# Agent attention with a token expert on one core: rank triangles made on GpSimd, ten key tiles, and a new order of the program

## The chip, the core and the metric

The kernel runs on one core of a Trainium2 chip. The metric is the device time of one execution in microseconds; of the kernel before there are three runs, and the changed kernel is compared with it by such runs. Engines are named as in the profile: PE (TensorE matmul), PEld (its weight load), DVE (VectorE), ACT (ScalarE), POOL (GpSimd), SP (SyncE, which here issues nearly all transfers).

## The reference

Four batches of 12608 tokens with 128 channels pass through agent attention with 49 agents, and then the 128 best tokens of each batch pass through an expert.

```python
def sm(a, b):
    s = scale * (a @ b.transpose(0, 2, 1))
    s = s - s.max(-1, keepdims=True)
    e = np.exp(s)
    return e / (e.sum(-1, keepdims=True) + 1e-09)
a2k = sm(agents, k)              # 49 x 12608
agent_v = a2k @ v                # 49 x 128
q2a = sm(q, agents)              # 12608 x 49
x = q2a @ agent_v                # 12608 x 128
...
scores = np.einsum('bsd,d->bs', x, w_gate)
out = x.copy()
for b in range(B):
    top_idx = np.argpartition(-scores[b], capacity)[:capacity]   # capacity = 128
    xe = x[b, top_idx]
    h = np.maximum(xe @ w1, 0.0)          # w1: 128 x 1024
    ye = h @ w2                           # w2: 1024 x 128
    g = 1.0 / (1.0 + np.exp(-scores[b, top_idx]))
    out[b, top_idx] = x[b, top_idx] + g[:, None] * ye
```

## The kernel before

**Tiles and stages.** Each batch is cut into seven chunks of tokens, six of 1920 and one of 1152. For a chunk of keys the transposed keys (`xT_b_c<-kT`) are loaded, and PE multiplies them with the agents (`S`, eight f32 matmuls of 480 columns, each counted twice in the trace, since an f32 matmul runs as two). DVE transposes the result into a key tile `sk` and takes the maximum `mx`. When all seven chunks of a batch are there, POOL subtracts the maximum and ACT takes the exponential in place, in `sk`. Then the values `v_b_c` are loaded and PE sums `sk` times `v` over the batch (`av`, one PSUM bank for each batch); `v_finish` divides and splits the result into fp16 halves `ws` (its matmuls are `pw` and `pp`). For the queries the transposed chunk is loaded and scored in the same way (`S`, DVE `sq` and `qm`); POOL, ACT, POOL make fp16 halves `f`, PE turns them (`fT`), ACT copies them out (`ft`), PE computes the gate scores (`pg`). When a batch is gated, its 128 best tokens are found and ranked: DVE and ACT count (`gt`) and PE broadcasts and sums (`all`, `pc`). The output is `po`, PE's product of `ft` and `ws`, four tokens of a partition at a time; DVE, ACT or ACT and POOL move it into `og_b_c`, which one transfer stores. The expert of batches 0 to 2 and that of batch 3 run among the last outputs (`ph`, `py`), and an indirect transfer writes their rows over the stored output.

**What sets the order.** Nothing is scheduled by the compiler. Every operation is recorded (`Recorder`), and `ORDER`, a list of 1466 numbers in lines 252 to 327, says in which order the operations are issued; `place` only asserts that each comes behind what it depends on. So the list sets, for each engine, the order of its instructions, and for SP the order of transfers. In the trace every such instruction has the line of that loop, L1123.

**Buffers.** All loads of k, q and v take a slot of the pool `inp` (`N_IN = 6`). A load is issued on SP when PE has done its last matmul on the tile that had the slot before, and whatever stands behind it on SP waits with it. Key tiles `sk` take a slot of `skp` (`N_SK = 9`), as do the two large pieces of the expert's weights (`w1_held`, `w2_held`) and the turned queries of batch 3. The outputs of batch 0 (`FILL`) have two slots of their own (`N_OG = 2`); the other 21 outputs use the six slots of `inp` once the loads have left them, and a new `og` waits there until the store of the `og` before it has landed.

**Constants.** `cst` is one transfer of 128x562 f32 (tenth on SP); a block of 128 columns in it is `tri`, ones above the diagonal. DVE casts it to bf16 as `tri_b` (L456), and adds the identity for `tri_i` (L462). Both serve only in the ranking of the best tokens, as weights of `pc`. `wg_sb`, the gate's vector, is the thirtieth transfer on SP, and `v_finish` is its first user; the matmul `pw` there is the first to use `cst` on PE.

```python
def load(src, name, w):
    t = inp.tile([P, TMAX * (C + 1)], F32, tag="in", name=name)
    nc.sync.dma_start(t[:, :w], src)
...
s = skp.tile([P, TMAX, AP_], F32, tag="sk", name=f"sk_{b}_{c}")
...
order, done = [rec.ops[i] for i in ORDER], set()
```

Of the kernel before, what the change touches and what calls it, by code (L numbers as in the profile page):

```python
# [24 lines left out]
P = 128  # L25
# [33 lines left out]
N_SK = 9  # L59
# [46 lines left out]
class Recorder:  # L106
# [1095 lines left out]
```

## Time and profile before

| | |
|---|---|
| runs | 287.15, 287.21 and 285.31 us, median 287.15 us |
| profiled execution | 285.31 us, span 283.4 us, granted clock 0.993 |
| busy, share of the span | PE 91%, PEld 62%, DVE 80%, ACT 60%, POOL 65% |
| moved | 106.68 MB, mean 376 GB/s |

The profiled execution is the fastest of the three. The span runs from its first to its last event; the 1.9 us between span and time lie around it. A name such as `v_2_1` means batch 2, chunk 1; the trace leaves the numbers out, the order of the program has them.

### The profile page before, as it was taken

Reading aid. Unit: us, or ns where it says so; the run is one execution under the profiler, and the core shown is the slowest. Engines: PE = TensorE matmul, PEld = TensorE weight load, DVE = VectorE, ACT = ScalarE, POOL = GpSimd, SP = SyncE. Lnnn points to the kernel's source line nnn. Section 1 sums busy time; section 2 is a strip of 40 time slices with the busy share of each in tenths; the row PEclk is TensorE's granted clock in tenths of the full one; section 3 lists DMA queues with packets and bytes.
Section 4 is the critical chain, followed back from the end, with each engine's and each line's share of the span. In section 5 each row is a group of like instructions: output and inputs, shape, how many; then the busy total and the mean of one; then the engine's idle time right before and its main releaser. Section 6 shows DMA issues by size and latency. Waiting matters only on the chain.

```text
span 283.4 us, 8570 instructions
## 1 busy us (share of the span) xinstructions
PE 258.7 (91%) x3524; PEld 175.7 (62%) x3524; DVE 226.3 (80%) x517; ACT 171.3 (60%) x313; POOL 183.8 (65%) x152
## 2 busy tenths in 40 slices
PE   1866699999999999999999999999999999999991
PEld 0211236556555756464575955866987989889980
DVE  0799999987999988999948979766954889997630
ACT  1103148454249965466685987998998865965510
POOL 1219699984489996358988418999426242568751
PEclk9999999999999999999999999999999999999997
DMA  7999999999999999999999999999644999899980
GB/s 278 426 424 417 421 423 415 418 421 421 417 419 417 398 416 418 383 384 417 421 423 416 378 423 425 411 408 421 208 198 139 344 376 411 351 415 380 417 332 27
DMA packets 18204, 106.68 MB, mean 376 GB/s; under 512 B 2032, under 2 KB 3440, under 8 KB 18160
## 3 DMA queue, kind: packets, MB, share of 16 engines
q1 hardware_dynamic: 17760, 105.42, 91.9%
q8 instruction: 30, 0.49, 0.7%
q0 software_dynamic: 256, 0.52, 0.6%
q10 hardware_dynamic: 144, 0.13, 0.1%
q14 instruction: 14, 0.11, 0.1%
HBM read 79.85 MB, written 26.21 MB: 374 GB/s over the span
## 4 chain that ended last, share of the span: by engine, by line
PE 64%; DMA 17%; DVE 9%; issue 3%; POOL 3%; ACT 1%; POOLq 0%; DVEq 0%
PE S L1123 23%; PE po L1123 13%; PE av L1123 10%; DMA v<-va 9%; DMA xT<-kT 6%; PE fT L1123 5%; PE pg L1123 3%; PE all L1123 3%; PE py L1123 3%; PE ph L1123 2%; DVE gt L1123 2%; DMA ag_sb<-agT 2%; DVE sk L1123 2%; DVE sq L1123 2%; DVE qm L1123 1%
## 5 line engine op out<-in xcount | busy, mean ns | idle before, releaser
L1123 PE MATMUL S<-xT,ag_sb 128*32 128x480 f32 (+1 forms) x896 | 97.8, 557 | 14.1 <-DMA ag_sb<-agT 6.1
L1123 POOL TENSOR_TENSOR sq<-sq,qm 128x735 f32<-128x735 f32 (+1 forms) x42 | 57.1, 1365 | 32.6 <-DVE qm L1123 31.1
L1123 PEld LDWEIGHTS <-ft 128*128 128x128 f16 x1188 | 57.9, 97 | 9.3 <-issue 8.4
L1123 PEld LDWEIGHTS S<-xT,ag_sb 128*32 128x32 f32 x896 | 24.4, 110 | 60.3 <-issue 25.8
L1123 POOL TENSOR_TENSOR f<-sq,f 128x735 f16<-128x735 f32 (+1 forms) x28 | 42.7, 1526 | 18.9 <-ACT f L1123 16.3
L1123 PE MATMUL po<-ws,ft 128*128 128x128 f16 x792 | 52.4, 219 | 0.5 <-ACT x L1123 0.4
L1123 ACT COPY ft<-fT 128x896 f16<-128x896 f16 (+2 forms) x49 | 42.9, 894 | 13.9 <-PE fT L1123 13.9
L1123 POOL TENSOR_TENSOR sk<-sk,mb 128x735 f32<-128x735 f32 (+1 forms) x28 | 47.3, 1701 | 6.2 <-DVE rs L1123 5.3
L1123 PE MATMUL av<-v,sk 128*64 128x129 f32 x792 | 47.8, 274 | 1.1 <-DMA v<-va 1.1
L1123 PEld LDWEIGHTS av<-v,sk 128*64 128x64 f32 x792 | 44.1, 136 | 7.6 <-issue 2.4
L1123 DVE STREAM_TRANSPOSE sq<-S 128x480 f32<-128x480 f32 (+1 forms) x56 | 34.5, 633 | 11.7 <-PE S L1123 11.5
L1123 DVE TENSOR_REDUCE qm<-sq 128x15 f32<-128x735 f32 (+1 forms) x42 | 36.0, 865 | 2.8 <-ACT sq L1123 2.2
L1123 ACT ACTIVATE sq<-sq,lift 128x735 f32<-128x735 f32 (+1 forms) x28 | 24.9, 888 | 19.3 <-POOL sq L1123 19.2
L1123 DVE STREAM_TRANSPOSE sk<-S 128x480 f32<-128x480 f32 (+1 forms) x56 | 35.0, 636 | 1.9 <-PE S L1123 1.8
L1123 POOL TENSOR_TENSOR og<-og,r 128x512 f32<-128x512 f32 (+1 forms) x26 | 23.9, 944 | 17.0 <-ACT og L1123 13.6
L1123 DVE TENSOR_REDUCE mx<-S 128x1 f32<-128x480 f32 (+1 forms) x56 | 33.1, 606 | 2.1 <-PE S L1123 1.7
L1123 PEld LDWEIGHTS <-f 128*128 128x128 f16 x396 | 22.9, 98 | 13.8 <-issue 9.8
L1123 PE MATMUL fT<-idh,f 128*128 128x128 f16 x396 | 28.7, 219 | 0.7 <-POOL f L1123 0.6
L1123 ACT CAST f<-sq 128x735 f16<-128x735 f32 (+1 forms) x28 | 22.0, 786 | 10.3 <-POOL sq L1123 9.5
L1123 ACT ACTIVATE sk<-sk 128x735 f32<-128x735 f32 (+1 forms) x28 | 22.0, 792 | 9.0 <-POOL sk L1123 9.0
L1123 DVE SCALAR_TENSOR_TENSOR gt<-all,top,minus 128x512 bf16<-128x512 f32 x32 | 23.7, 742 | 2.4 <-PE all L1123 1.8
L1123 ACT ACTIVATE gt<-all,top 128x512 bf16<-128x512 f32 x32 | 22.0, 687 | 3.1 <-PE all L1123 2.6
(131 smaller groups left out, 244.6 us busy)
## 6 DMA issues: line engine op xcount, KB each, us to landing
v<-va SPq DMA_DIRECT2D x24, 967.5 KB, 9.0
xT<-qT SPq DMA_DIRECT2D x24, 960.0 KB, 9.1
xT<-kT SPq DMA_DIRECT2D x24, 960.0 KB, 9.3
out<-og SPq DMA_DIRECT2D x24, 960.0 KB, 6.1
v<-va SPq DMA_DIRECT2D x4, 580.5 KB, 8.1
xT<-kT SPq DMA_DIRECT2D x4, 576.0 KB, 7.5
xT<-qT SPq DMA_DIRECT2D x4, 576.0 KB, 7.6
out<-og SPq DMA_DIRECT2D x4, 576.0 KB, 7.0
```

Source lines behind the costliest of these rows:

```text
L1123: call(*args, **kwargs)
```

## The change

The `tri` block leaves `cst` (now 128x434). `tri_b` and `tri_i` are made on POOL by `make_upper_triangular`, each a MEMSET and an AFFINE_SELECT, and DVE's cast and addition go. `N_SK` becomes 10. `ORDER` is replaced as a whole: the same operations (with four instructions of POOL for two of DVE), 3524 matmuls as before, in another order on every engine. The title's weight of the experts' products belongs to the search that made the list, and is not in the kernel.

```diff
-from concourse.masks import make_identity
+from concourse.masks import make_identity, make_upper_triangular
...
-N_SK = 9
+N_SK = 10
...
 ORDER = (
...
 )
...
-        "tri": P,
...
-    c[:, slice(*at["tri"])] = np.triu(np.ones((P, P), np.float32), 1)
...
     tri_b = const.tile([P, P], BF16, name="tri_b")
-    nc.vector.tensor_copy(tri_b, cs("tri"))
+    make_upper_triangular(nc, tri_b, diag=False)
...
     tri_i = const.tile([P, P], BF16, name="tri_i")
-    nc.vector.tensor_tensor(tri_i, cs("tri"), idf, op=ALU.add)
+    make_upper_triangular(nc, tri_i)
```

PE, ahead of the sum over the second chunk of values of batch 2 (`av_2` on `v_2_1`). Names end in a running number; `po_0_3_4` is an output of batch 0, chunk 3, from its fourth token on. Before:

```order
L1123 LDWEIGHTS ft_0_1_178
L1123 MATMUL po_0_1_12_644<-ws_0_160,ft_0_1_178 128x128
L1123 MATMUL S_3_3_0_517<-xT_3_3_516,ag_sb_91 32x480 x4
L1123 MATMUL S_3_3_1_518<-xT_3_3_516,ag_sb_91 32x480 x4
L1123 MATMUL av_2_407<-v_2_1_408,sk_2_1_376 64x129 x15
L1123 LDWEIGHTS ft_0_3_196
L1123 MATMUL po_0_3_0_651<-ws_0_160,ft_0_3_196 128x128
```

and now:

```order
L1121 LDWEIGHTS ft_0_3_196
L1121 MATMUL po_0_3_4_652<-ws_0_160,ft_0_3_196 128x128
L1121 MATMUL S_3_4_1_522<-xT_3_4_520,ag_sb_91 32x480 x4
L1121 MATMUL S_2_5_1_471<-xT_2_5_469,ag_sb_91 32x480 x4
L1121 MATMUL S_2_5_0_470<-xT_2_5_469,ag_sb_91 32x480 x4
L1121 MATMUL av_2_407<-v_2_1_408,sk_2_1_376 64x129 x15
L1121 LDWEIGHTS ft_0_3_196
L1121 MATMUL po_0_3_8_653<-ws_0_160,ft_0_3_196 128x128
```

The outputs `po_0_3_0` and `po_0_3_4` (16 matmuls) and the query scores of `S_2_5` (two halves, 16 matmuls as the trace counts them) now stand ahead of that `av`; before, they came behind it.

SP, the last loads and the first stores behind them (`v_3_6` is the last load of v; a load's size is given as partitions x f32 elements). Before:

```order
L1123 DMA out0<-og_0_5_660 128x1920
L1123 DMA v_3_2_540<-va 128x1935
L1123 DMA v_3_3_541<-va 128x1935
L1123 DMA v_3_4_542<-va 128x1935
L1123 DMA xT_3_5_600<-qT 128x1920
L1123 DMA v_3_5_543<-va 128x1935
L1123 DMA v_3_6_544<-va 128x1161
L1123 DMA out1<-og_1_0_669 128x1920
L1123 DMA w1_held_633<-w1 128x896
L1123 DMA w2_held_634<-w2 128x7x128
L1123 DMA out0<-og_0_4_655 128x1920
L1123 DMA out0<-og_0_6_665 128x1152
```

and now:

```order
L1121 DMA v_3_2_540<-va 128x1935
L1121 DMA w1_held_633<-w1 128x896
L1121 DMA v_3_4_542<-va 128x1935
L1121 DMA v_3_3_541<-va 128x1935
L1121 DMA xT_3_5_600<-qT 128x1920
L1121 DMA v_3_5_543<-va 128x1935
L1121 DMA v_3_6_544<-va 128x1161
L1121 DMA out0<-og_0_5_660 128x1920
L1121 DMA out0<-og_0_4_655 128x1920
L1121 DMA out1<-og_1_0_669 128x1920
L1121 DMA out0<-og_0_6_665 128x1152
L1121 DMA w2_end_95<-w2 128x128
```

The store of `og_0_5` went from ahead of the last loads to behind them, `og_0_4` follows it, `og_1_0` comes third instead of first, and `w1_held` is loaded among the last values.

SP around the thirtieth transfer, before and now:

```order
L1123 DMA xT_1_1_247<-kT 128x1920
L1123 DMA wg_sb_93<-wgb 128x128
L1123 DMA xT_1_6_267<-kT 128x1152
L1123 DMA xT_1_1_303<-qT 128x1920
```

```order
L1121 DMA xT_1_1_247<-kT 128x1920
L1121 DMA cst_92<-consts 128x434
L1121 DMA xT_1_6_267<-kT 128x1152
L1121 DMA xT_1_1_303<-qT 128x1920
```

`cst` and `wg_sb` have changed places: `wg_sb` is now the first transfer on SP, and `cst` the thirtieth.

## Rows read from the trace of the kernel before

**Rows 1.** Page, part 1: busy us, share of span, instructions.
```profile
PE 258.7 (91%) x3524; PEld 175.7 (62%) x3524; DVE 226.3 (80%) x517; ACT 171.3 (60%) x313; POOL 183.8 (65%) x152
```

**Rows 2.** Windows by stage; the first line names the columns.
```profile
core 0: us, PE busy (x) PEld busy (x) DVE busy (x) ACT busy (x) POOL busy (x), PEclk, DMA share, GB/s
0.00:40.00 40.00, 25.52 (x226) 7.28 (x226) 29.69 (x57) 7.21 (x10) 20.00 (x21) 1.00 0.97 396
40.00:145.00 105.00, 102.71 (x1390) 60.68 (x1385) 96.32 (x209) 65.48 (x111) 82.60 (x61) 1.00 1.01 413
145.00:200.00 55.00, 54.65 (x818) 38.86 (x816) 42.52 (x102) 46.17 (x82) 40.14 (x31) 1.00 1.00 405
200.00:218.00 18.00, 17.45 (x288) 15.78 (x284) 11.88 (x39) 16.75 (x32) 8.97 (x7) 1.00 0.50 173
218.00:277.00 59.00, 58.18 (x823) 53.05 (x820) 45.54 (x111) 35.68 (x82) 31.15 (x33) 1.00 0.94 372
```

**Rows 3.** Lines by form, PE, 40 to 145 us: xcount, busy us, mean ns, idle.
```profile
L1123 PE MATMUL S<-xT,ag_sb 128*32 128x480 f32 x431 | 48.9, 571 | 1.1 <-DMA xT<-kT 1.1
L1123 PE MATMUL av<-v,sk 128*64 128x129 f32 x448 | 27.5, 275 | 1.1 <-DMA v<-va 1.1
L1123 PE MATMUL fT<-idh,f 128*128 128x128 f16 x190 | 13.7, 220 | 0.0
...
L1123 PE MATMUL pg<-ws,ft 128*128 128x3 f16 x159 | 5.1, 167 | 0.0
```

**Rows 4.** Chain that ended last, in order of time: start us, us, what.
```profile
68.03 0.37 PE pw L1123 x2
...
134.35 9.33 DMA v<-va
143.82 1.95 PE av L1123 x30
...
156.67 6.76 PE av L1123 x120
...
184.30 3.36 PE S L1123 x32
...
190.70 1.42 PE pg L1123 x54
...
195.02 0.94 PE fT L1123 x15
...
255.21 4.81 PE po L1123 x84
```

**Rows 5.** Timeline of SP, two stretches: start us, us, transfer issued.
```profile
58.52 0.43 SPq L1123 DMA_DIRECT2D wg_sb<-wgb  x1
...
202.25 2.07 SPq L1123 DMA_DIRECT2D v<-va  x2
216.31 0.34 SPq L1123 DMA_DIRECT2D out<-og  x1
```

**Rows 6.** DMA issues, whole span: xcount, KB each, median us to landing.
```profile
wg_sb<-wgb SPq DMA_DIRECT2D x1, 64.0 KB, 10.0
```

**Rows 7.** DMA issues of windows 190 to 225, 120 to 146, 218 to 277 us.
```profile
xT<-qT SPq DMA_DIRECT2D x1, 960.0 KB, 4.8
...
out<-og SPq DMA_DIRECT2D x1, 960.0 KB, 9.1
...
out<-og SPq DMA_DIRECT2D x18, 960.0 KB, 5.9
```

**Rows 8.** Tiles idf, tri_b, tri_i: xcount, ns min/median/max, first and last start us.
```profile
L1123 POOL MEMSET idf<- x1: 205/205/205, 1.2 to 1.2; 128x128 f32 x1
L1123 POOL TENSOR_SCALAR_AFFINE_SELECT idf<-idf x1: 288/288/288, 26.8 to 26.8; 128x128 f32<-128x128 f32 x1
...
L1123 DVE CAST tri_b<-cst x1: 467/467/467, 65.5 to 65.5; 128x128 bf16<-128x128 f32 x1
L1123 DVE TENSOR_TENSOR tri_i<-cst,idf x1: 286/286/286, 100.3 to 100.3; 128x128 bf16<-128x128 f32 x1
```

148 rows, old and new, of the table ORDER are left out of this document.

## The prediction

> **What bounds the kernel now.** I read the windows by stage first, because one average hides four regimes [rows 2]. To 40 us PE is busy 25.5 us and DVE, which must transpose every score, 29.7. From 40 to 145 us PE shows 102.7 of 105 us, but the DMA share is 1.01 at 413 GB/s. From 200 to 218 us DMA falls to 0.50 and 173 GB/s while PE still shows 17.45 of 18. From 218 to 277 us PE shows 58.2 of 59, its weight loads 53.1, and DMA 0.94.
>
> A busy PE is not a PE at its peak, since a matmul that has little behind it is shown long: the lines give 571 ns for a score matmul [rows 3]. So I take what a matmul costs where PE works without a gap, from long pieces of the chain of waits [rows 4]: S 3.36/32 = 0.105 us, `av` 6.76/120 = 0.056, `fT` 0.94/15 = 0.063, `pg` 1.42/54 = 0.026, `po` 4.81/84 = 0.057. In the stage from 40 to 145 us that makes 431 x 0.105 + 448 x 0.056 + 190 x 0.063 + 159 x 0.026 = 86.6 us [rows 3], and for the 162 other matmuls of its 1390 [rows 2] at about 0.07 another 11.3: some 98 of 105 us. About 7 us are lost there. Those rows name the cause: what idle time there is ended with DMA, 1.1 us with `kT` and 1.1 with `va`. In the tail no such gap is left to win: `po` follows `po` on the chain.
>
> The mechanism in that stage is a slot's turnaround. A load goes out when PE leaves its slot and lands some 9 us later, 9.33 for `v_2_1` [rows 4]. PE must have that much other work between the two. For `v_2_1` it has, by the order before, 56 S, 14 `po` and 30 `fT`: 5.9 + 0.8 + 1.9 = 8.6 us. That is 0.8 too little, and `av` starts as the load lands, at 143.82 [rows 4]. That is the last place where the chain goes through a load; everything behind is work of PE or what PE hands on.
>
> **The change, part by part.**
>
> *Order ahead of `v_2_1`.* The new order puts two `po` groups and both halves of `S_2_5` before that `av`. Between the slot's release and the use there are now 64 S, 30 `po`, 30 `fT`: 6.7 + 1.7 + 1.9 = 10.3 us, more than 9.33, so this wait goes. In all, PE has 16 S and 16 `po` more behind it at this point, 16 x 0.105 + 16 x 0.057 = 2.6 us. What is late next is the transfer itself: counted along SP, 57.62 MB stand up to `v_2_1` instead of 57.29, and 0.33 MB at 413 GB/s is 0.8 us [rows 2]. So 2.6 us less work is left behind a point that comes 0.8 us later: **-1.8 us**. Bounds: 0, if another wait holds the same work up; -7, all that the stage loses.
>
> *Other turnarounds.* The load before it, `v_2_0`, gains 3 us of cover (8.5 to 11.8) and `k_2_4` 2.3 (7.4 to 9.7). Others take a shorter place: `q_1_6` 7.5, `k_2_6` 6.8, `k_2_5` 7.8. All of these lie ahead of `v_2_1`, whose DMA stream catches them up as long as SP is never empty, so I count nothing for them beyond its 0.8 us; if that cover is gone, each costs its lack against 9.3, at most 2.5. Of the loads behind the first `v` of batch 1, 22 had under 9 us before and 14 have now.
>
> *`v_3_3`.* It takes the slot of `q_3_6`: between are only 16 S, 16 `all` and 60 `av`, 6.9 us, where before it had 13.6. With the 4.8 us that the last query load took it costs nothing, with the 9.33 of `v_2_1` 2.4 [rows 4, 7]. `w1_held` now runs just ahead of it on SP, so I take a fifth, **+0.5 us**, since DMA is on its way to the 0.50 of the next stage.
>
> *Triangles.* POOL gets two MEMSETs and two AFFINE_SELECTs on 128x128: the identity's cost 0.205 and 0.288 us [rows 8], so 2 x 0.493 = 1.0 us; DVE loses 0.467 + 0.286 = 0.75 us. POOL shows 82.6 of 105 us in that stage, DVE 96.3 [rows 2]: neither is full, PE has 9 us of work behind each of their results, and the triangles are needed only at the first ranking. Net 0, bounds -0.75 and +1.0. The 64 KB less of `cst` are 0.16 us of a stage whose DMA is full, and lie within the 0.8 above.
>
> *`cst` thirtieth, `wg_sb` first.* In that place `wg_sb` was issued at 58.52 us [rows 5] and landed 10.0 us later [rows 6], while `pw`, the first matmul on `cst`, stood at 68.03 [rows 4]: 0.5 us too late for it, and `cst` is larger. Bounds 0 and 2. The loss lies ahead of `v_2_1`, where PE waits anyway, so it counts nothing. `wg_sb` ahead of the first load: 64 KB, under 0.5 us, while PE waits for the agents in any case.
>
> *Stores.* SP stood still from the last `v` at 202.25 to 216.31 [rows 5] behind the store of `og_1_0`. Now `og_0_5` and `og_0_4` stand in that place, 1.97 MB, 4.8 us at 413 GB/s [rows 2]. They come out of a later stretch that DMA does not bound by my reading: 0, bounds 0 and -4.8.
>
> *Tenth key tile.* It moves key scores earlier and adds no work; all it does is in the order already counted.
>
> Sum: -1.8 + 0.5 = -1.3 us on the profiled execution's 285.31 (span 283.4 and 1.9 around it), 284.0. That execution is 1.84 us under the median of the three, so a median of new runs should lie above such a sum; I add half of it, 0.9, here and to each rival: **284.9 us**. About 1%, 2.9 us, is what a measurement of this kernel can tell: faster means under 284.3, slower over 290.0.
>
> **The rivals.**
>
> *The hole is what counts.* If DMA and not PE sets the tail, the 4.8 us of stores that fill the hole come off the end in full, with the 1.8: 285.31 - 4.8 - 1.8 + 0.9 = 279.6 us. For it: 0.94 of DMA from 218 us on, and 14 us without an issue [rows 2, 5]. Against it: PE shows 58.2 of 59 us there, weight loads 53.1, and the chain has `po` upon `po` [rows 2, 4]. For the whole span the weight loads' share is only 62% [rows 1]. The Trainium skill, "Perfetto Trace Analysis", section "Identifying the Most-Contended Engine", says that matmul busy time is no measure of how full TensorE is and that the share of weight loads is one; read over the span that rule would leave TensorE headroom and give this rival's 279.6, read over the last stage (53.1/59, 90%) it gives mine. That does not alter the sum. Chance 0.25, which also holds the lesser form in which only part of the hole is won.
>
> *The waits only move.* The short turnarounds named above, or DVE's order in the first 40 us, take back what `v_2_1` gives, by as much as 1.3 us: no change, 285.31 + 0.9 = 286.2. For it: every load of that stage lives within 1 or 2 us of its landing. Chance 0.20.
>
> *Stores too slow for the slots, slower.* In the tail an `og` waits in its slot of `inp` for the store before it to land. The new order brings some closer: between the last `po` of `og_1_1` and the first of `og_3_0`, its heir, PE has 5.5 us of work (56 `po`, 45 `pg`, 15 `fT` and three small ones); before `og_2_6` it has 7.1, before `og_3_4` 7.9. The tightest before were 6.7 and 7.2. Stores there landed in 5.9 us in the median, but the one issued while DMA was full, from 120 to 146 us, took 9.1 [rows 7]. At 9.1 the three lose 3.6 + 2.0 + 1.2 = 6.8 us: 284.9 + 6.8 = 291.7. It passes 290.0 where a store takes 8.5 us (3.0 + 1.4 + 0.6 = 5.0 us). Early stores in the hole make the tail's DMA less full, which speaks against it. Chance 0.13.
>
> That the change does not do what it says is no case here: the order of SP and PE shows each move.
>
> **How the numbers follow.** Forecast, two waits gone and nothing else: 0.42, with a range of its own of 282.5 to 287.5 (the bounds of `v_3_3`, of `cst` and of half the stage's 7 us). Its predicted time is 284.9. Faster by over 1%: 0.13 of the forecast's 0.42, 0.23 of the hole's 0.25 and 0.02 of the moved waits: 0.38. Slower: 0.11 of the slots' 0.13 and 0.03 from the rest: 0.14. Within: 0.48. The range for 8 in 10 goes from 279.5, which takes in the hole's case, to 290.0.
>
> **What would show it.** Right: in the profile after, no piece of the chain is a load of `va` that ends at the `av` of `v_2_1`; PE's stage to 145 us holds more matmuls; S and `po` beside loads show shorter means. The hole from 202 to 216 us is filled and the span ends only a little earlier: PE still 98% busy behind 218 us. The forecast is wrong if the chain runs through a load behind 150 us (`v_3_3`, `v_3_5`, `v_3_6`), through DVE or POOL where the triangles stand, or if `po` in the tail shows idle time that ended with a store; and if PE's busy time behind 218 us falls by as much as the hole is filled, it was DMA that set the tail.

## The result and the profile after

The changed kernel takes 282.73 us (median of 20 runs, 281.66 to 285.53), the kernel before 285.75 us (20 runs, 284.99 to 287.61): ratio 0.9898, 95% interval 0.9873 to 0.9923, so 1.0% or some 3 us faster. The forecast of 284.9 us lies 2.2 us above the measured time, which is inside the range of 279.5 to 290.0. Ratios here and below leave out executions that ran visibly longer than the others of the same kernel, among them two of six in the run on the stores and two of twelve (334 and 641 us) in the run with the new order up to 166 us. The profiled execution took 281.66 us, its span is 279.9 us, 3.5 us shorter than before.

The windows by stage of the changed kernel, to be laid beside [rows 2]:

```profile
core 0: us, PE busy (x) PEld busy (x) DVE busy (x) ACT busy (x) POOL busy (x), PEclk, DMA share, GB/s
0.00:40.00 40.00, 28.63 (x242) 8.23 (x242) 30.11 (x60) 8.23 (x11) 19.68 (x20) 1.00 0.97 396
40.00:145.00 105.00, 102.34 (x1377) 61.12 (x1377) 94.26 (x205) 64.26 (x112) 82.78 (x66) 1.00 1.01 409
145.00:200.00 55.00, 54.67 (x833) 39.72 (x827) 43.65 (x107) 47.96 (x80) 41.92 (x33) 1.00 1.01 409
200.00:218.00 18.00, 17.96 (x289) 15.84 (x285) 12.83 (x40) 17.68 (x39) 8.30 (x7) 1.00 0.78 287
218.00:277.00 59.00, 56.30 (x799) 51.85 (x795) 42.87 (x107) 33.86 (x75) 31.98 (x33) 1.00 0.85 340
```

By 145 us PE has issued 1619 matmuls, before 1616: the stage in which I looked for the gain gives next to nothing. The first 40 us hold 16 more, but 40 to 145 us hold 13 fewer. The waits of PE from 40 to 145 us (engine and tile, waited for: us, times, longest) show why, first the kernel before, then the changed one:

```profile
PE av L1123 <- DMA v<-va: 1.1, 3, 0.5
PE S L1123 <- DMA xT<-kT: 1.1, 2, 0.7
```

```profile
PE mB L1121 <- ACT ft L1121: 0.6, 1, 0.6
PE S L1121 <- DMA xT<-qT: 0.6, 1, 0.6
PE S L1121 <- DMA xT<-kT: 0.3, 1, 0.3
PE av L1121 <- DMA v<-va: 0.3, 1, 0.3
PE S L1121 <- DVE iv L1121: 0.3, 1, 0.3
PE pw L1121 <- DVE sq L1121: 0.2, 1, 0.2
```

The waits for loads went from 2.2 to 1.2 us, and 1.1 us of waits for ACT and DVE came up, 2.3 us in all (the old order shows 1.3 us in the profile of the first run below): they moved.

The pause of DMA from 200 to 218 us is half filled (0.78 instead of 0.50). A finer cut behind 166 us shows where the two part. The kernel before:

```profile
166.00:190.00 24.00, 23.65 (x336) 15.73 (x333) 18.68 (x48) 21.01 (x37) 18.64 (x14) 1.00 1.02 416
190.00:218.00 28.00, 27.45 (x445) 23.12 (x443) 18.78 (x54) 25.45 (x46) 17.76 (x14) 1.00 0.65 246
218.00:230.00 12.00, 11.63 (x200) 10.31 (x198) 10.11 (x21) 10.14 (x21) 3.24 (x3) 1.00 0.97 342
```

The changed kernel, same columns:

```profile
166.00:190.00 24.00, 23.90 (x348) 16.31 (x345) 17.90 (x46) 18.51 (x31) 19.93 (x16) 1.00 1.02 422
190.00:218.00 28.00, 27.76 (x453) 23.38 (x450) 21.00 (x59) 27.36 (x54) 16.01 (x13) 1.00 0.85 319
218.00:230.00 12.00, 12.00 (x250) 11.64 (x247) 8.85 (x19) 10.02 (x18) 3.87 (x3) 1.00 0.71 265
```

In each stretch PE gets more matmuls done: 12, 8 and 50 more. To compare mixes of matmuls I price them at their closest spacing in the trace (S 0.101 us, `av` 0.0565, `po` and `fT` 0.056, `pg` 0.027, the others likewise) and call the time that passed beyond that price PE's loss. Loss in us, worked out for each profile (old order: before, and three runs of the experiments below that keep it):

```
stretch      before  e1_tri  e2_sk10  b_dve2 | after  a_plus
150 to 166    0.35    0.69    0.41     0.35  | 0.60   0.60
166 to 190    2.60    2.27    2.64     2.61  | 2.06   2.07
190 to 218    2.48    2.84    2.46     2.86  | 1.78   1.73
218 to 230    1.10    1.13    1.19     1.16  | 0.22   0.25
150 to 230    6.54    6.92    6.70     6.97  | 4.66   4.65
```

Some 1.9 us of the gain are made there (6.54 to 4.66). The chain of waits has changed with it. Before, it left PE from 197.8 to 215.8 us for DVE, POOL and their issue:

```profile
203.38 1.16 DVE sq L1123 x2
...
206.16 1.44 POOL sq L1123
207.59 4.10 issue
...
213.21 0.95 POOL xq L1123
...
214.18 1.62 POOL f L1123
```

Now it stays on PE there:

```profile
31.77 9.34 DMA xT<-qT
...
47.52 10.44 DMA v<-va
...
97.42 10.75 DMA xT<-kT
...
145.76 1.91 PE av L1121 x30
...
204.60 0.61 PE fT L1121 x9
205.21 0.34 PE po L1121 x6
...
207.44 0.93 PE fT L1121 x15
```

PE's waits from 165 to 232 us, before and after, tell the same:

```profile
PE fT L1123 <- POOL f L1123: 0.6, 2, 0.3
PE po L1123 <- ACT x L1123: 0.4, 1, 0.4
PE fT L1123 <- ACT ft L1123: 0.2, 1, 0.2
```

```profile
PE S L1121 <- issue: 0.2, 1, 0.2
```

The last load on the chain is now `k_2_4`'s, which ends at 108.2 us; neither `v_2_0` nor `v_2_1` stands on it any more [rows 4]. But the sum over `v_2_1` starts at 145.76 us, not at the 144.6 of my sum. On SP the stores follow the last loads at once, where before nothing was issued until 216.31 [rows 5]:

```profile
199.78 3.63 SPq L1121 DMA_DIRECT2D v<-va  x2
203.50 16.09 SPq L1121 DMA_DIRECT2D out<-og  x4
```

Stores of the tail land as fast as before [rows 7], and a triangle's AFFINE_SELECT costs what the identity's did (0.301 and 0.288 us) [rows 8]:

```profile
out<-og SPq DMA_DIRECT2D x17, 960.0 KB, 5.8
```

```profile
L1121 POOL TENSOR_SCALAR_AFFINE_SELECT tri_b<-tri_b x1: 301/301/301, 93.5 to 93.5; 128x128 bf16<-128x128 bf16 x1
```

The rest of the difference lies at the very end. DMA in the last 5.5 us of the span, before (277.9 to 283.4 us) and after (274.4 to 279.9 us). The last indirect store (the expert's rows of batch 3) starts at 277.9 us before and at 275.4 after; the last line gives its landing, the q14 line the instruction fetches of 8 KB:

```profile
q14 instruction: 3, 0.02, 2.0%
...
out<-ey,idx POOLq DMA_INDIRECT x1, 3.5
```

```profile
q14 instruction: 2, 0.02, 0.9%
...
out<-ey,idx POOLq DMA_INDIRECT x1, 2.4
```

The last store lands in 3.5 us before and in 2.4 after, and there is one instruction fetch less. The same store, the same 64 KB: 1.1 us that no engine's work explains. So 3.5 us of span are 1.1 at the end, 1.9 between 150 and 230 us, and 0.5 ahead of 150 us, which the next runs show to be within the spread of the old order's own profiles.

### The profile page after: what moved, and what is told of

The parts are those of the page before. It is cut to its first block, busy times and chain, and to the rows that moved or that the text cites. A ratio compares the mean times of both kernels' runs of the same rounds, so it can differ in the third digit from the quotient of the medians.

```text
span 279.9 us, 8582 instructions
## 1 busy us (share of the span) xinstructions
PE 259.9 (93%) x3524; PEld 176.8 (63%) x3524; DVE 223.7 (80%) x515; ACT 172.0 (61%) x313; POOL 184.7 (66%) x156
## 4 chain that ended last, share of the span: by engine, by line
PE 73%; DMA 16%; DVE 6%; issue 2%; ACT 1%; POOL 1%; POOLq 0%; SPq 0%
PE S L1121 22%; PE po L1121 16%; PE av L1121 14%; DMA xT<-kT 8%; PE fT L1121 6%; DMA xT<-qT 5%; DMA v<-va 4%; PE pg L1121 3%; PE all L1121 3%; PE py L1121 3%; PE ph L1121 2%; DVE mx L1121 2%; DVE sk L1121 1%; DVE qm L1121 1%; DVE sq L1121 1%
## 5 line engine op out<-in xcount | busy, mean ns | idle before, releaser
L1121 DVE TENSOR_SCALAR og<-po,iv 128x512 f32<-128x512 f32 (+1 forms) x26 | 17.6, 681 | 8.1 <-PE po L1121 5.8
```

Source lines behind the costliest of these rows:

```text
L1121: call(*args, **kwargs)
```

## The experiments

Two theories stood against each other. Theory 1, the prediction's: the loads up to `v_2_1`. Theory 2: waits of PE for DVE, ACT and POOL behind 150 us. Ratios are to the kernel before, which ran on the same chip beside each run. `old` and `new` stand for the two lists of numbers.

**The triangles alone.** All but `ORDER` and `N_SK` of the change; `ORDER` is the old one with POOL's four instructions in the place of DVE's two.

```diff
-    nc.vector.tensor_copy(tri_b, cs("tri"))
+    make_upper_triangular(nc, tri_b, diag=False)
...
-    nc.vector.tensor_tensor(tri_i, cs("tri"), idf, op=ALU.add)
+    make_upper_triangular(nc, tri_i)
```

> The order of before, nine key tiles, and only the triangles made on POOL (their four instructions at the place of DVE's two, cst 128 columns narrower). My sum put this part at 0, bounds -0.75 and +1.0 us: ratio 1.000, between 0.997 and 1.0035. A rival that gives the gain to the triangles and the smaller constant expects the ratio of the whole change, 0.990 (about -2.9 us). PE's start of the second chunk of values of batch 2 stays at 143.8 us within 0.3.

Measured 0.9964 (0.9930 to 0.9997), about 1.0 us, a third of the whole gain from a part that I had put at 0. PE loses as much as before; the last store lands as in the changed kernel.

**A tenth tile with the old order.**

```diff
-N_SK = 9
+N_SK = 10
```

> The run before this one with ten key tiles and still the old order. If a tile more were worth something by itself, since a load of key scores or of weights then finds a slot earlier, the ratio falls to 0.995 or less; by my reading the order alone uses it, and the ratio is that of the run with nine, within 0.002.

Measured 0.9961 (0.9934 to 0.9989), the same as with nine within the interval: the tile by itself shows no gain.

**Two instructions fewer on DVE, nothing else.**

```diff
-    nc.vector.memset(lift, math.log(FSCALE))
+    nc.gpsimd.memset(lift, math.log(FSCALE))
...
-    nc.vector.memset(eps, 1e-9)
+    nc.gpsimd.memset(eps, 1e-9)
```

> The kernel before in everything (its order, nine key tiles, triangles loaded and made on DVE), but two one-column memsets of the set-up (lift and eps) moved from DVE to POOL, so that DVE's stream is two instructions shorter, as it is with the triangles on POOL. Theory A, code position: in the profile of before DVE's branch at the end is its 576th instruction, an 8 KB instruction fetch starts 1.57 us after the last indirect store is issued, and that store's last packet ends 1.0 us later than in the kernels without this fetch; so here the fetch is gone, the end stands 4.4 us behind the last indirect store instead of 5.5, and the ratio is 0.996 to 0.997 as with the triangles alone. Theory B, the triangles' own work or the smaller constant: ratio 1.000, and 5.5 us.

Measured 0.9966 (0.9944 to 0.9987). The triangles are still loaded and made on DVE, and yet the gain is as large as theirs. DMA in the last 5.5 us of this run (277.7 to 283.2 us):

```profile
q14 instruction: 2, 0.02, 1.2%
...
out<-ey,idx POOLq DMA_INDIRECT x1, 2.4
```

Two fetches and 2.4 us, as in the changed kernel. So the microsecond of the triangles is not their work, nor the smaller constant, but the place of DVE's last instructions in its stream.

**Both halves of the order, cut at the sum over `v_2_1`.** `ORDER` is the first 719 operations of the new list and then all others as the old list has them; and the other way round, with the first 698 of the old.

```diff
-ORDER = new
+ORDER = new[:719] + [op for op in old if op not in new[:719]]
```

> Ten key tiles, triangles on POOL; the new order up to PE's sum over v_2_1 (about 147 us), behind it all that is left in the order of before. Theory 1, the prediction's: the gain is made by the loads ahead of that sum, so all or most of it is here: ratio 0.990 to 0.994. Theory 2: behind 145 us the old order makes PE wait for ACT and POOL at hand-overs, and the new order has fewer of these; only the 0.8 us by which PE is ahead at 145 us shows here: ratio 0.997.

> The counterpart: the order of before up to PE's sum over v_2_1, behind it what is left in the new order. Theory 1: little or nothing, ratio 0.998 to 1.000, and the load of v_2_1 still ends a piece of the chain. Theory 2: most of the gain, ratio 0.991 to 0.994, with PE's losses behind 145 us as in the changed kernel (6 us or less of its idle and stretched time instead of 8).

Measured 1.0199 (1.0167 to 1.0231) and 1.0046 (1.0012 to 1.0080): both slower (1.1 us of the latter are the third fetch described at the end). At this cut one list has issued loads and key scores that the other hasn't, and the first run's PE stands still for 4.4 us ahead of a `pg` at 152.34 us, for a `ft` of ACT. The times tell nothing of either theory, but that the loads' order and the engines' belong together. The losses tell a little: from 190 to 230 us the second run, which has the new order there, loses some 1.5 us less than the kernel before, as the changed kernel does, the first run only 0.4 less.

**The prediction's first term done alone.** Old order, triangles on POOL; on PE:

```diff
 L1121 MATMUL S_3_3_1_518<-xT_3_3_516,ag_sb_91 32x480 x4
-L1121 MATMUL av_2_407<-v_2_1_408,sk_2_1_376 64x129 x15
 L1121 LDWEIGHTS ft_0_3_196
 L1121 MATMUL po_0_3_0_651<-ws_0_160,ft_0_3_196 128x128
...
 L1121 MATMUL po_0_3_4_652<-ws_0_160,ft_0_3_196 128x128
+L1121 MATMUL av_2_407<-v_2_1_408,sk_2_1_376 64x129 x15
```

> The order of before with the triangles on POOL and nine key tiles, and one move: PE's sum over v_2_1 goes behind po_0_3_0, three pg, fT_2_1 and po_0_3_4, 2.9 us of PE's work. It is the prediction's first term done alone. Theory 1: the wait of some 0.8 to 1.2 us ahead of that sum goes, PE stands 0.7 to 1.8 us better behind 150 us and at the end: ratio 0.990 to 0.994 to the kernel before. Theory 2: v_2_1's landing is no longer waited for, but the slot it leaves 2.9 us later makes a load behind it late by as much as was won: 0.995 to 0.998.

Measured 1.0095 (1.0065 to 1.0125), 3.7 us slower than the same kernel without the move (0.9964), of which 1.1 come from the fetch at the end; 2.6 us are the move's. PE's waits from 143 to 163 us, its chain there, and a window of this run:

```profile
PE pg L1121 <- ACT ft L1121: 0.6, 2, 0.4
PE po L1121 <- ACT og L1121: 0.4, 1, 0.4
PE S L1121 <- DVE sk L1121: 0.2, 1, 0.2
```

```profile
146.00 1.71 ACT ft L1121 x2
...
151.03 3.12 PE av L1121 x30
```

```profile
143.00:150.00 7.00, 5.99 (x103) 4.04 (x100) 4.44 (x9) 6.97 (x11) 5.04 (x4) 1.00 1.01 420
150.00:154.00 4.00, 3.98 (x38) 3.67 (x37) 0.00 (x0) 2.38 (x3) 3.90 (x3) 0.57 0.78 325
```

The wait for `v_2_1` is gone, but the work that was put ahead of the sum waits in its place: the `pg` for a `ft` and the `po` for an `og` of ACT, which is busy for 6.97 of the 7.00 us. Behind these waits the granted clock is 0.57 from 150 to 154 us, the lower of its two levels for most of that time, and the 30 `av` of the sum take 3.12 us instead of the changed kernel's 1.91. The loads behind the slot are late too: SP takes 11.2 us for the three next loads of `v`, before 6.2, since `v_2_3` waits for the sum. But no wait of PE in that window ends with a load. The profiled execution took 291.19 us, the kernel's five others 287.16 to 289.58, so how the 2.6 us divide in those is open. I had asked what is late next only of the transfer ahead of the sum, not whether the work put there would be ready.

**One wait of POOL taken away.** Old order, triangles on POOL; on POOL:

```diff
+L1121 TENSOR_TENSOR f_3_1_568<-sq_3_1_563,f_3_1_568 128x15x49
+L1121 TENSOR_TENSOR f_3_3_586<-sq_3_3_581,f_3_3_586 128x15x49
 L1121 DMA xq_0_0_771<-q2,idx_2_501 128x128
 L1121 DMA xq_0_0_771<-q1,idx_1_370 128x128
-L1121 TENSOR_TENSOR f_3_1_568<-sq_3_1_563,f_3_1_568 128x15x49
-L1121 TENSOR_TENSOR f_3_3_586<-sq_3_3_581,f_3_3_586 128x15x49
```

> The order of before with the triangles on POOL and nine key tiles (as in the first run), and one move: the gathers xq of batches 2 and 1 on POOL go from ahead of the low halves f of q_3_1 and q_3_3 to behind them. Theory 2: POOL waits 4.3 us for the indices of the gather and holds those halves up, PE then waits at fT_3_1 (0.5 us) and those behind it; moved, PE's loss between 205 and 232 us falls from 2.7 to 2.2 us or less, and the ratio to the kernel before goes from 0.9964 to 0.993 to 0.995. Theory 1 (loads) expects the first run's time again, 0.996.

Measured 0.9963 (0.9932 to 0.9995), no gain to be told from the 0.9964 without the move. The halves do come 2.7 us earlier on POOL (210.70 instead of 213.35), and the 0.5 us around `fT_3_1` are gone from PE's losses, but the other waits stay (0.97 us ahead of `fT_3_0`, 0.37 ahead of `fT_3_5`) and 190 to 218 us come to 2.42, within the spread of the old order's profiles. One hand-over mended alone is too little to be seen.

**Both halves of the order, cut where the lists agree.** At 820 operations (some 166 us) the two prefixes differ in ten operations only, so that I expected the seam to cost little.

```diff
-ORDER = new
+ORDER = new[:820] + [op for op in old if op not in new[:820]]
```

> Ten key tiles, triangles on POOL; the new order up to some 166 us (where the two orders have done nearly the same operations), behind it what is left in the order of before. Theory 1 (the loads ahead of v_2_1): most of the order's gain, some 1.9 us against the old order with triangles on POOL, so 0.990 to the kernel before. Theory 2 (waits of PE for other engines between 166 and 230 us): the same as the old order with triangles on POOL, 0.995 to 0.998, and PE loses 6 to 7 us between 150 and 230 us as there. With a branch of DVE at place 575 or later 1.05 us are added to either.

```diff
-ORDER = new
+ORDER = old[:820] + [op for op in new if op not in old[:820]]
```

> The counterpart: the order of before up to some 166 us, the new one behind. Theory 2: PE loses 4.7 us instead of 6.6 between 150 and 230 us, and the ratio is 0.989 to 0.992 to the kernel before (without the fetch at the end). Theory 1: 0.996.

Measured 1.0010 (0.9971 to 1.0049) for new then old, 0.9868 (0.9816 to 0.9920) for old then new. The old first half with the new second half has the whole gain. The new first half shows none, but there the seam is not cheap: PE waits 1.4 us for a load of q, ahead of `S_2_4` at 170.0 us. Without that wait the run would stand at the old order's 0.996, within an interval of 0.4% to either side, so theory 1's further 1.9 us are not there. PE from 190 to 230 us in the latter run:

```profile
190.00:218.00 28.00, 27.90 (x462) 24.09 (x460) 20.18 (x59) 27.20 (x53) 17.28 (x13) 1.00 0.82 306
218.00:230.00 12.00, 11.97 (x229) 10.93 (x226) 8.20 (x17) 10.33 (x19) 3.23 (x3) 1.00 0.71 265
```

462 and 229 matmuls where the kernel before has 445 and 200, and a DMA of 0.82 and 0.71 as in the changed kernel. Its loss from 190 to 230 us is 2.0 us (1.55 and 0.48), with the old order 3.6 to 4.0.

**The last part of the new order alone**, cut at 1110 operations (some 216 us).

```diff
-ORDER = new
+ORDER = old[:1110] + [op for op in new if op not in old[:1110]]
```

> The order of before up to some 216 us (fT_3_1), the new one behind. In the profiles PE loses 1.2 us between 218 and 230 us with the old order and 0.3 with the new one: theory 2 expects 0.9 us of the gain here, 0.993 to 0.994, and the rest from the stretch between 166 and 216 us. If the whole of theory 2's gain were made by the stores that fill the pause of SP from 202 to 216 us, nothing would be gained here: 0.996.

Measured 0.9975 (0.9941 to 1.0009): no gain to be seen against the 0.9961 of the old order with ten tiles. This run's PE loses some 0.7 us more between 218 and 230 us than the kernel before, right behind the seam, so that what the last part gives by itself is not shown. The gain needs the stretch from 166 to 216 us in the new order too, or a seam that costs nothing.

**The stores.** The changed kernel with one edit on SP:

```diff
 L1121 DMA v_3_6_544<-va 128x1161
+L1121 DMA out1<-og_1_0_669 128x1920
 L1121 DMA out0<-og_0_5_660 128x1920
 L1121 DMA out0<-og_0_4_655 128x1920
-L1121 DMA out1<-og_1_0_669 128x1920
```

> The changed kernel with one edit on SP: the store of og_1_0 goes first behind the last load again, ahead of those of og_0_5 and og_0_4, as before. DMA then stands idle for some 10 us longer around 210 us and carries 1.97 MB, 4.8 us, more behind 218 us. My prediction counted nothing for the stores: 0.990, within 0.002 of the changed kernel. The rival that DMA sets the tail: 4.8 us given back, 1.006; a part of it, 0.995, if batch 0's outputs wait for their two slots.

Measured 1.0120 (1.0042 to 1.0198), 6 us slower than the changed kernel, more than DMA's bytes can cost. The first stores on SP, PE's wait and two windows of this run:

```profile
217.53 10.74 SPq L1121 DMA_DIRECT2D out<-og  x4
```

```profile
PE po L1121 <- ACT og L1121: 5.0, 1, 5.0
```

```profile
200.00:218.00 18.00, 17.97 (x291) 16.34 (x290) 13.42 (x43) 17.58 (x39) 9.28 (x7) 1.00 0.48 173
218.00:277.00 59.00, 53.98 (x784) 48.68 (x782) 42.16 (x102) 35.86 (x80) 27.36 (x30) 0.94 0.89 358
```

PE stands still once, for 5.0 us at 219 us, ahead of `po_0_6_4`: ACT cannot empty the bank, since `og_0_6` needs one of batch 0's two slots and neither `og_0_5` nor `og_0_4` has been stored. DMA's share behind 218 us is 0.89, under the 0.94 of the kernel before: DMA is not full in the tail even here. The granted clock's mean falls to 0.94 in that stretch (0.59 from 224 to 230 us), behind the 5 us without work.

**A further move**, on the changed kernel: `xe` of batch 3's expert ahead of the last `py` of the first group, on PE, and what hangs on it on DVE and ACT.

```diff
 L1121 MATMUL py_0_795<-w_end,hT_0_0_792 128x128
+L1121 MATMUL xe_0_807<-wfs,ey_0_805 128x129
 L1121 MATMUL py_0_795<-w_held,hT_0_0_783 128x128 x2
...
 L1121 MATMUL ph_3_0_812<-xT_0_808,w_end 128x128
-L1121 MATMUL xe_0_807<-wfs,ey_0_805 128x129
 L1121 MATMUL py_0_813<-w_held,hT_3_0_809 128x128 x4
```

> The changed kernel with one further move in the last 10 us: xe of batch 3's expert, its copy to bases and the gate's exp, add and reciprocal go ahead of the last py of the first group. In the changed kernel the last py waits 0.38 us for that copy behind ph, and xe itself stands in between; so the last py should start about 0.9 us earlier and the whole end by as much: 0.987 instead of 0.990 to the kernel before. If the last store of batch 3, and not PE, set the end, nothing is gained.

Measured 0.9900 (0.9866 to 0.9934), the changed kernel's 0.9898 within the interval. The last `py` starts 0.3 us earlier (272.43 instead of 272.73): only the wait goes, while `xe` itself, which I had counted as won, is PE's work at any place. None of the runs beats the changed kernel clearly.

## Why the prediction held, and which of its steps did not

The direction, the place in the range and the case "no load but work of PE sets the end" held: 284.9 forecast, 282.73 measured. The sum did not come out of the right terms, and that is luck: it promised 1.3 us, and the 3 us measured are 1.0 at the end of the program and some 1.9 of hand-overs, neither of which it held.

- *`v_2_1`, -1.8 us: wrong.* The wait went, as the chain shows, but the sum starts at 145.76 us, 1.1 us later than I had it, and the stage to 145 us does not hold more matmuls, as I had asked for: 1377 instead of 1390 from 40 us on. By 145 us the new order is 0.8 us ahead of the profiled execution before, and of the same old order in the run with the triangles alone by nothing. New order up to 166 us shows no gain, and the move alone costs 2.6 us. The failing step is "I count nothing for them" of the other turnarounds: the waits moved ahead of `v_2_1`, to `q_0_5` (0.6 us at 41.2 us) and `v_0_4` (0.3 at 58.0), neither of them among the loads that I named, and to hand-overs of ACT and DVE (1.1 us), which no load's cover touches. In this stage the rival "the waits only move" was right, and the term came to its lower bound of 0.
- *`v_3_3`, +0.5 us: within its bounds.* No load behind 108 us is on the chain, so 0 and not a fifth of 2.4.
- *`cst` thirtieth: 0, held.* It was issued at 58.09 us, `pw` came at 68.50; the 0.2 us that PE waits ahead of it are for DVE, and at 70 us PE's loss is that of the kernel before within 0.3 us.
- *Triangles, net 0 between -0.75 and +1.0: wrong by 1.0 us*, 0.9964, and for a reason that no term of a sum over work could hold (the run with two instructions fewer, 0.9966).
- *Stores, 0: the size held, the reason not.* Filling the pause gave nothing through DMA: its share behind 218 us fell from 0.94 to 0.85 while PE stayed full (56.3 us of the 56.8 to its last matmul), and PE's busy time there fell by 1.9 us, not by the 5 us of DMA's time (0.28 of 18 us) that the pause took up. So the rival "the hole is what counts" fell. But the place of these stores is worth 6 us in the other direction, through batch 0's two slots; before, `og_0_5` was stored ahead of the last loads, and that order had no such wait. The Trainium skill's rule on weight loads ("Perfetto Trace Analysis", "Identifying the Most-Contended Engine"), that their busy share and not that of the matmuls is to be read, agrees if it is read over the last stage, as the prediction did (53.1 of 59 us there, 51.9 now); read over the span it does not.
- *Left out: hand-overs behind 150 us, about -2.* I wrote that in the tail "no such gap is left to win", from `po` upon `po` on the chain, with PE busy at 17.45 of 18 and 58.2 of 59 us. Yet those rows hide waits of 0.3 to 0.6 us each: a `po` is shown with 0.219 us in the mean where the next one can follow after 0.056, so PE looks busy over most of a short wait. In the kernel before they stand ahead of `po_0_2_12` (0.53), `fT_3_0` (0.63), `fT_3_6` (0.34), `fT_3_1` (0.51) and `fT_3_5` (0.39). The four `fT` turn batch 3's queries, which POOL and ACT make; the `po` waits for ACT. The chain told it too: from 197.8 to 215.8 us it went through DVE, POOL and their issue, not through PE. In the changed kernel none of these five is left over 0.25 us.
- *The slots of the tail, slower: did not come.* Stores landed in 5.8 us, far from the 8.5 from which it would have decided.

Which of the new order's moves between 166 and 216 us does it is not settled: the one that I took out of it shows no gain by itself, and the joined orders show only that the new order behind 166 us as a whole does it. That the five waits are what it saves is read from the profiles, where loss and waits fall together; no run took them away alone.

## What to carry to other kernels

Price each matmul at its closest spacing and take the loss by stretch: a row that shows PE 97% busy can hide as much as one with a gap, and the piece of the chain that leaves PE says where. When other work is put ahead of a use to cover its load, ask first whether that work will be ready, and add up the waits of the whole stage before counting the one that goes. Before a microsecond is credited to an edit, give the kernel an edit of the same number of instructions with nothing in it.

## What the runs showed of the hardware

The end of this program has two lengths. In eleven profiles with DVE's closing branch as the 572nd to 575th or the 577th of its instructions in the trace, the span ends 4.4 to 4.6 us after the start of the last indirect store. In three (before, and two of the runs: the second half of the new order behind `v_2_1`, and `v_2_1`'s sum moved alone) it is the 576th; the branch comes 0.36 us later, a third 8 KB instruction fetch starts 1.5 to 1.7 us after the store, takes 0.6 to 0.7 us, and the store's last packet ends at 2.8 instead of 1.9 us, the span at 5.5. That the fetch holds up the store's last packets is argued from these times. That the place in DVE's stream decides it is shown by the run that only took two instructions from it: they went to POOL, but POOL's branch is the 224th instruction in runs with the third fetch and without it. It is the place and not a length from which on the fetch comes, as I had expected in one run ("place 575 or later"): at the 575th and the 577th there is none.
